# Strassen's scheme for the first FFN product beside attention, with weight sums streamed from DRAM

## The chip, the cores and the metric

One core of a Trainium2 chip. The metric is the device time of one execution, in microseconds (us), of that core. I write PE for TensorE, ACT for ScalarE, DVE for VectorE, POOL for GpSimd and SP for SyncE, as the profile does.

## The reference

Attention with a threshold over 8 sequences of 8 heads (576 x 64), then a feed-forward network (FFN) with ELU on the 4608 tokens, all in fp32:

```python
scores = scale * np.matmul(q, k.transpose(0, 1, 3, 2))
thresh = np.max(scores, axis=-1, keepdims=True) - tau
scores = np.where(scores >= thresh, scores, -1000000000.0)
attn = np.exp(scores - np.max(scores, axis=-1, keepdims=True))
attn = attn / (np.sum(attn, axis=-1, keepdims=True) + 1e-09)
attn_out = np.matmul(attn, v)
# ... (heads are put side by side: x is 4608 x 512)
h = x @ w_in                                        # 512 -> 2048
g = np.where(h > 0.0, h, np.exp(np.minimum(h, 0.0)) - 1.0)
return g @ w_out                                    # 2048 -> 512
```

## The kernel before

Heads are worked in pairs, 32 of them (four per sequence). The FFN of a group of 512 finished tokens fills PE while the attention of later pairs waits for softmax. A pair has five steps. In each, PE makes scores; DVE takes the maximum, ACT the exponential, DVE masks and sums, POOL normalizes; DVE turns 32 x 32 squares of the weights into a tile `x`, and SP writes it to DRAM and reads it back as the transposed weights for the product with v.

```python
    def turn_squares(pr, i):
        w = open_steps.pop((pr, i))["w"]
        x = late["x"].tile([P, NT, NCH, T], FP32, name="x", bufs=2)
        # ... (DVE: nc.vector.transpose, 3 to 4 times)
        there = turns[pr, i] = dram.tile([NT, T, NT, NCH * T], FP32, name="there")
        for p in range(NT):
            nc.sync.dma_start(there[:, :, p]..., x[p * T : (p + 1) * T]...)
```

Beside attention the first FFN product is plain: 4 matmuls into a bank, and only then exponential, minus one, ELU.

```python
        def part(k):
            ft = fts[k]
            if k == 0:
                loc["ph"] = psum["f"].tile([P, 2, CT], FP32, name="ph", tag="f")
            for j in range(KJ):
                nc.tensor.matmul(loc["ph"][:, k], w_in_sb[:, j, ft * P : (ft + 1) * P],
                                 xts[g][:, j, hf * CT : (hf + 1) * CT], start=(j == 0), stop=(j == KJ - 1))
```

The second product uses Strassen's scheme (7 products of half-blocks in place of 8, for some additions) already. In the final stage, after attention, both products do.

## Time and profile before

| | before |
|---|---|
| time, median of 3 (range) | 1424.34 us (1419.48 to 1424.73) |
| span of the profiled execution | 1418.1 us |
| PE busy / idle | 1373.6 / 44.5 us |
| a pair of heads beside attention, pairs 11 to 30, alternately | 37.7 and 38.6 us |
| moved by DMA | 204 MB, 144 GB/s |

The idle time is the span less PE's busy time. A pair is measured from the start of its first scores to that of the next pair's; the "pairs" below alternate between those in which the changed kernel does a first product ("first pairs") and a second product ("second pairs"). One more line of the page matters, the chain that ended last, followed back from the end:

```profile
PE 84%; DVE 8%; ACT 3%; POOL 2%; issue 2%; SPq 0%; DMA 0%; DVEq 0%; POOLq 0%
```

A chain that is 84% PE says that nearly everything else lay beside PE's work.

### The profile page before, as it was taken

Reading aid. Unit: us, or ns where it says so; the run is one execution under the profiler, and the core shown is the slowest. Engines: PE = TensorE matmul, PEld = TensorE weight load, DVE = VectorE, ACT = ScalarE, POOL = GpSimd, SP = SyncE. Lnnn points to the kernel's source line nnn. Section 1 sums busy time; section 2 is a strip of 40 time slices with the busy share of each in tenths; the row PEclk is TensorE's granted clock in tenths of the full one; section 3 lists DMA queues with packets and bytes.
Section 4 is the critical chain, followed back from the end, with each engine's and each line's share of the span. In section 5 each row is a group of like instructions: output and inputs, shape, how many; then the busy total and the mean of one; then the engine's idle time right before and its main releaser. Section 6 shows DMA issues by size and latency. Waiting matters only on the chain.

```text
span 1418.1 us, 20448 instructions
## 1 busy us (share of the span) xinstructions
PE 1373.6 (97%) x6758; PEld 1024.1 (72%) x6758; DVE 950.5 (67%) x2070; ACT 449.2 (32%) x812; POOL 669.4 (47%) x1170
## 2 busy tenths in 40 slices
PE   6897989999999999999999999999999999999998
PEld 4455645657777777777777777777777777788887
DVE  6878884667676767676776767676767767563542
ACT  5676654223232322232232323232323222120220
POOL 5566774646363544545353626354544445241330
PEclk9999999999999999999999999999999999999999
DMA  5254451567666767767676767667776765100001
GB/s 112 56 98 138 127 145 41 142 166 189 188 188 181 192 183 192 193 184 184 180 190 180 193 183 192 183 183 189 192 193 170 201 174 170 59 0 15 15 1 30
DMA packets 298905, 205.45 MB, mean 145 GB/s; under 512 B 206384, under 2 KB 270384, under 8 KB 298800
## 3 DMA queue, kind: packets, MB, share of 16 engines
q1 hardware_dynamic: 298800, 204.15, 53.9%
q8 instruction: 54, 0.88, 0.3%
q14 instruction: 51, 0.42, 0.1%
HBM read 119.87 MB, written 84.21 MB: 144 GB/s over the span
## 4 chain that ended last, share of the span: by engine, by line
PE 84%; DVE 8%; ACT 3%; POOL 2%; issue 2%; SPq 0%; DMA 0%; DVEq 0%; POOLq 0%
PE ph L434 26%; PE po L539 24%; PE sc L236 12%; PE pv L386 9%; PE po L868 7%; DVE w L263 3%; ACT e L251 3%; PE po L503 2%; PE pv L382 2%; DVE mx L246 2%; PE rt L275 1%; POOL wtop L142 1%; DVE wtop L136 1%; POOL nb L247 1%; DVE wtop L135 1%
## 5 line engine op out<-in xcount | busy, mean ns | idle before, releaser
L434 PE MATMUL ph<-xt,w_in_sb 128*128 128x256 f32 x1792 | 406.7, 382 | 0.0
L434 PEld LDWEIGHTS ph<-xt,w_in_sb 128*128 128x128 f32 x1792 | 335.2, 190 | 64.0 <-issue 20.5
L251 ACT ACTIVATE e<-sc,nb,keep 128x576 f32<-128x576 f32 x288 | 227.4, 829 | 473.6 <-POOL nb L247 472.6
L246 DVE TENSOR_REDUCE mx<-sc 128x2 f32<-128x1152 f32 (+1 forms) x176 | 199.7, 1136 | 234.6 <-PE sc L236 234.6
L272 POOL TENSOR_SCALAR w<-w,rs 128x576 f32<-128x576 f32 x288 | 224.3, 789 | 224.7 <-DVE rs L266 216.8
L263 DVE SCALAR_TENSOR_TENSOR w<-sc,th,e 128x576 f32<-128x576 f32 x288 | 226.2, 815 | 78.5 <-ACT e L251 54.9
L236 PE MATMUL sc<-kT,qT 64*128 64x288 f32 x1024 | 181.1, 439 | 22.4 <-DVE w L263 12.0
L346 DVE STREAM_TRANSPOSE x<-w 128x512 f32<-128x512 f32 (+1 forms) x350 | 181.1, 566 | 0.9 <-POOL w L272 0.9
L247 POOL TENSOR_SCALAR nb<-mx,nkeep 128x2 f32<-128x2 f32 (+1 forms) x176 | 51.2, 291 | 261.7 <-DVE mx L246 253.8
L236 PEld LDWEIGHTS sc<-kT,qT 64*128 64x128 f32 x1024 | 99.9, 190 | 87.3 <-issue 52.4
L539 PE MATMUL po<-t,s 128*128 128x256 f32 x512 | 122.8, 386 | 4.5 <-DVE u L559 4.5
L539 PE MATMUL po<-w_out_sb,s 128*128 128x256 f32 x512 | 120.1, 384 | 0.0
L539 PEld LDWEIGHTS po<-t,s 128*128 128x128 f32 x512 | 94.6, 190 | 28.9 <-DVE u L559 8.9
L539 PEld LDWEIGHTS po<-w_out_sb,s 128*128 128x128 f32 x512 | 95.4, 190 | 19.7 <-issue 4.7
L442 ACT ACTIVATE g<-ph 128x512 f32<-128x512 f32 x112 | 66.9, 597 | 126.0 <-PE ph L434 126.0
L539 PE MATMUL po<-w_out_sb,g 128*128 128x256 f32 x448 | 103.2, 379 | 0.0
L445 POOL TENSOR_SCALAR g<-g 128x512 f32<-128x512 f32 x112 | 70.0, 625 | 66.8 <-ACT g L442 65.8
L539 PEld LDWEIGHTS po<-w_out_sb,g 128*128 128x128 f32 x448 | 85.1, 190 | 12.2
L449 DVE SCALAR_TENSOR_TENSOR g<-g,ph 128x512 f32<-128x512 f32 x112 | 74.8, 669 | 18.2 <-POOL g L445 18.1
L471 POOL TENSOR_TENSOR s<-g 128x256 f32<-128x256 f32 x112 | 82.7, 739 | 3.9 <-DVE g L912 3.9
L386 PE MATMUL pv<-wTb,vm 128*64 128x320 f32 x512 | 78.1, 448 | 0.0
L393 ACT COPY xt<-pv 128x256 f32<-128x256 f32 x64 | 23.8, 371 | 155.5 <-PE pv L386 155.5
(161 smaller groups left out, 1512.7 us busy)
## 6 DMA issues: line engine op xcount, KB each, us to landing
there<-x SPq DMA_DIRECT2D x500, 144.0 KB, 3.4
wTb<-there SPq DMA_DIRECT2D x75, 576.0 KB, 4.5
wTa<-there SPq DMA_DIRECT2D x50, 576.0 KB, 3.7
qm<-in_q_dram SPq DMA_DIRECT2D x128, 72.0 KB, 2.7
km<-in_k_dram SPq DMA_DIRECT2D x128, 72.0 KB, 3.7
vm<-in_v_dram SPq DMA_DIRECT2D x64, 128.0 KB, 2.5
wst<-in_moe_w_in_dram SPq DMA_DIRECT2D x16, 512.0 KB, 4.6
wst<-in_moe_w_out_dram SPq DMA_DIRECT2D x16, 512.0 KB, 4.2
```

Source lines behind the costliest of these rows:

```text
L236: nc.tensor.matmul(scs[h][:, a, :HALF], qs[r], kT[r, k0 : k0 + HALF], start=True, stop=True)
L246: nc.vector.tensor_reduce(st["mx"][:, cs], src[:, :, :, :HALF], axis=AX.XY, op=ALU.max)
L251: nc.scalar.activation(e, st[h][:, :, :HALF], AF.Exp, bias=st["nb"][:, h : h + 1], scale=keep)
L263: nc.vector.scalar_tensor_tensor(wv, sc[:, :, :HALF], st["th"][:, h : h + 1], e, ALU.is_ge, ALU.mult, accum_out=sm[:, h : h + 1])
L272: nc.gpsimd.tensor_scalar(wv, wv, st["rs"][:, h : h + 1], 1.0, ALU.mult, ALU.mult)
L346: nc.vector.transpose(x[:, :, c0 : c0 + nc_], src.rearrange("p (c g n) -> p g c n", c=nc_, n=T))
L386: nc.tensor.matmul(pv[h * D : (h + 1) * D, g0 * T : g1 * T], vm[:, h, c], wT[:, g0:g1, h * (NC + 1) + c], start=False, stop=(c == NC - 1), ...
L434: nc.tensor.matmul(loc["ph"][:, k], w_in_sb[:, j, ft * P : (ft + 1) * P], xts[g][:, j, hf * CT : (hf + 1) * CT], start=(j == 0), stop=(j = ...
L449: nc.vector.scalar_tensor_tensor(loc["g"], loc["g"], 0.0, loc["ph"], ALU.min, ALU.max)
L471: engines[k].tensor_tensor(out, x, y, op)
L539: nc.tensor.matmul(cur[c, place], lhs, rhs, start=(begins and u == 0), stop=(u == NU - 1), skip_group_check=True)
L868: nc.tensor.matmul(place, left[:, k], right[:, k], start=(begins and k == 0), stop=(k == 1), skip_group_check=True)
```

## The change

The intent: 7 products instead of 8 in the first product beside attention as well. Sums of weight blocks are made once, written to DRAM and loaded again per unit, since there is no room for them. To save room the hidden features are done in two rounds of half of them. ACT copies three products out of PSUM in each unit, POOL and DVE add them, and an agenda sorted by planned time replaces the fixed order. Maxima, biases and exponentials go by head instead of by pair, with the bias of the exponential on ACT. The diff, cut:

```diff
     def turn_squares(pr, i):
         w = open_steps.pop((pr, i))["w"]
-        x = late["x"].tile([P, NT, NCH, T], FP32, name="x", bufs=2)
+        x = late["x"].tile([P, NT, NCH, T], FP32, name="x", bufs=1)
...
+            def product(k):
+                # ... (three banks; s: the sums loaded from DRAM)
+                left, right, place, begins = ((s[:, 0], x1, 0, True), (s[:, 1], b22, 1, True), (s[:, 2], b11, 2, True),
+                                              (a11, b12, 1, False), (a22, b21, 2, False), (a21, x6, 1, False),
+                                              (a12, x7, 0, False))[k]
+                for j in range(2):
+                    nc.tensor.matmul(loc["banks"][place], left[:, j], right[:, j], start=(begins and j == 0), stop=(j == 1),
+                                     skip_group_check=True)
...
+            after_ = (
+                [(0.1, lambda: copy("s1", 0))],
+                [(0.1, lambda: copy("w1", 1))],
+                [(0.1, lambda: copy("u2", 2)), ... (POOL sums) ...],
+                [(0.1, lambda: nc.scalar.copy(h(0, 1), place(1)))],
+                [(0.1, lambda: nc.scalar.copy(h(1, 0), place(2))), ...],
+                [(0.1, lambda: add(h(1, 1), 1, "s1")), *tail(1)],
+                [(0.1, lambda: add(h(0, 0), 0, "t5")), *tail(0)],
+            )            # tail(c): exp at +0.7 (ACT), minus one at +1.45 (POOL), ELU at +2.2 (DVE)
...
+        def softmax(pr, i):
+            t = clock[0]
+            on_pe(1.25, lambda: scores(pr, i, hs))
+            for h in hs:
+                at(t + 1.2 + 0.01 * h, lambda h=h: max_of(pr, i, h))
+                at(t + 2.0 + 0.75 * h, lambda h=h: bound_of(pr, i, h))
+                at(t + 2.1 + 0.8 * h, lambda h=h: exp_of(pr, i, h))
+                at(t + 3.1 + 0.85 * h, lambda h=h: mask_of(pr, i, h))
+            # ... (reciprocal, normalize)
+            at(t + 6.2, lambda: turn_squares(pr, i))
...
```

## The prediction

> **What bounds the kernel now.** I read the page first, its shares and its costliest groups:
>
> ```profile
> PE 1373.6 (97%) x6758; PEld 1024.1 (72%) x6758; DVE 950.5 (67%) x2070; ACT 449.2 (32%) x812; POOL 669.4 (47%) x1170
> ...
> L434 PE MATMUL ph<-xt,w_in_sb 128*128 128x256 f32 x1792 | 406.7, 382 | 0.0
> ...
> L251 ACT ACTIVATE e<-sc,nb,keep 128x576 f32<-128x576 f32 x288 | 227.4, 829 | 473.6 <-POOL nb L247 472.6
> ...
> L471 POOL TENSOR_TENSOR s<-g 128x256 f32<-128x256 f32 x112 | 82.7, 739 | 3.9 <-DVE g L912 3.9
> ```
>
> PE is busy 97% of the span. The costliest group is the plain first product, and no idle time stands before it. Then I read the busy times by stretch, over ten whole pairs of heads (from one transpose of kT to the tenth after it, so one pair takes 38.14 us):
>
> ```profile
> 312.50:693.90 381.40, 379.18 (x1921) 286.97 (x1922) 266.43 (x580) 108.12 (x180) 183.99 (x344) 1.00 0.69 187
> ```
>
> The columns are length, busy time of PE, weight loads, DVE, ACT and POOL, the granted clock, the DMA share and GB/s. PE idles 2.2 us in 381, so beside attention the time is PE's. DVE works 26.6 us per pair, ACT 10.8, POOL 18.4. Third, the timeline of one attention step, because the change puts work on ACT and DVE that PE waits for:
>
> ```profile
> 603.14 1.24 PE L236 MATMUL sc<-kT,qT 64*128 64x288 f32 x8
> ...
> 604.31 1.99 PE L539 MATMUL po<-t,s 128*128 128x256 f32 x8
> 604.42 1.36 DVE L246 TENSOR_REDUCE mx<-sc 128x2 f32<-128x1152 f32 x1 [3.27 <-PE sc L236]
> ...
> 605.88 0.27 POOL L247 TENSOR_SCALAR nb<-mx,nkeep 128x2 f32<-128x2 f32 x1 [3.40 <-DVE mx L246]
> ...
> 606.18 1.55 ACT L251 ACTIVATE e<-sc,nb,keep 128x576 f32<-128x576 f32 x2 [7.40 <-POOL nb L247]
> ```
>
> PE has left the scores 1.17 us after it began them, the maximum starts 1.28 us after, one engine follows another in about 0.1 us, and ACT then does two exponentials in 1.55 us without a gap. Today nothing on PE needs ACT in that time. Fourth, the final stage, which already runs Strassen's first product, with ACT free:
>
> ```profile
> 1226.14 1.03 PE L868 MATMUL po<-xt,w_in_sb 128*128 128x256 f32 x4
> ...
> 1227.01 1.03 PE L868 MATMUL po<-wTa,w_in_sb 128*128 128x256 f32 x4
> 1227.21 0.37 ACT L874 COPY s<-po 128x256 f32<-128x256 f32 x1 [0.56 <-PE po L868]
> ...
> 1227.87 1.03 PE L868 MATMUL po<-xt,w_in_sb 128*128 128x256 f32 x4
> ```
>
> The three PE rows are one product each (two matmuls, four records). They start 0.865 us apart, so a matmul of 256 columns costs 0.432 us. A bank can be read 1.07 us after its product began, a copy takes 0.37, and PE's next product in that bank, two products on, began 0.29 us after the copy ended. That is the whole slack of such a bank, and it needs an idle ACT.
>
> [...] I therefore count matmuls by their spacing (0.432 us). The trace agrees that busy time is not work: it gives 1792 records 382 ns each, which start about 216 ns apart. [...] The trace of before agrees: three banks hold three independent units and L434 idles 0.0. The change lets the seven products of one unit return to the same three banks. [...] here it is 0.73 us in the steady stretch against 0.42 on DVE for 256 columns.
>
> **The change, part by part.**
>
> PE, removed. A group of 512 tokens needs 128 matmuls in the first product, and by Strassen 8 units x 7 products x 2 = 112. Six groups lie beside attention (groups 7 and 8 used the scheme already): 6 x 16 x 0.432 = 41.5 us, or 1.7 us per pair, 3.4 us per two pairs. The count of the second product stays (two rounds of half its depth). If PE stayed the bound, the time were 1383.
>
> Engines, added per pair (a quarter of a group). DVE: 30 more additions of 256 columns per group (16 in the first product, 14 from the second in two rounds), 7.5 x 0.42 = 3.1; input sums 1.25 x 0.69 = 0.9; maxima by head 9 x 0.75 against 4 x 1.36 + 0.75, 0.6; ELU from SBUF, 0.4. Sum 5, so 31.5 us of 36.4: 86%. ACT: 10 copies x 0.37 = 3.7, nine small bias products x 0.2 = 1.8; 16.5 us. POOL: 7.5 x 0.73 = 5.5; 24 us. No engine passes PE on the average.
>
> Waits, added: this decides. Each unit writes banks 0, 1, 2, 1, 2, 1, 0. Before products 3, 4 and 5 ACT must have copied products 1, 2 and 3 out, each with the 0.29 us of slack above. Engines take instructions in program order, and the agenda sorts ACT's by planned time. A pair of heads is planned with 8, 6, 4, 6, 4 quarters (one product each) in its five steps, 28, exactly four units. So the phase is the same in each first-product pair, and I can write it out. With 0 at the scores' start: maximum of head 0 at 1.29 to 2.04, bias on ACT 2.14 to 2.34, exponential of head 0 to 3.19, then copy s1 to 3.5, bias and exponential of head 1 to 4.5, then copy w1 to 4.9. PE starts product k at 1.17 + 0.86 k.
> - Steps 0 and 2 (products 0 to 3 follow the scores): product 3 would start at 3.75, and must wait for w1 till about 5.0: 1.25 us each.
> - Step 1 (products 1, 2, 3, 4 first): product 3 waits for a copy behind the exponential of head 0, 3.6 against 2.9; product 4 for one behind that of head 1, 5.0 against 4.5: 1.25 together.
> - Step 3 begins with product 4, whose copies have time: 0. Step 4 begins with product 3, and product 5 waits for a copy behind its only exponential: 0.75.
> Sum 4.5 us per first-product pair, with a DVE that is never late. Half of the 24 pairs are such: 12 x 4.5 = 54 us, more than the 41.5 saved.
>
> On top, chosen rather than read off: an ELU that stands in DVE's order before the next maximum waits for POOL, which normalizes (2 x 0.75) before it serves the unit's sums. Written out for step 1 the maximum comes about 1.1 us late, and each such delay reaches PE through the exponentials. I take 1.5 us per first-product pair, 18 us. In second-product pairs, sums of the last unit queue on POOL behind the normalization: 0.5 us, 6 us. Two pairs between the stages in which PE has only the plain chunk while POOL and DVE make weight sums: 4 us. The final stage has as many matmuls as before and idled little (PE 48.5 of 50 us where it begins), so 0.
>
> Sum: 1424 - 41.5 + 54 + 18 + 6 + 4 = 1464.5, I say 1465.
>
> DMA: the sums of w_in are 128 x 768 x 4 bytes = 0.39 MB a unit, those of w_out 128 x 1024 x 4 bytes x 6 = 3.1 MB a group: 6.3 MB per group, 41 GB/s over 152 us on 187. Each is asked for several products ahead, in rows of 3 to 4 KB. I expect no PE wait on them.
>
> **Rivals.**
> 1. PE stays the bound and most of the 41.5 us arrives: 1385 to 1396. For it: the averages (DVE 86%, ACT 46%), scores in two banks by head, which ends the wait for the mask, and an order planned by time. Against it: the written-out steps, which use only durations of this trace and the program's order.
> 2. Only the floor of waits happens, DVE and POOL never add to it: 1424 - 41.5 + 54 = 1437, within 2%. For it: PE's stalls give the other engines time to catch up, so lateness cannot pile up.
> 3. DVE becomes the bound in first-product pairs: there it has 8 additions and 8 ELUs per pair rather than the mean, so about 33 us of work, and waits for POOL and ACT in its order. Then each step grows by about 2 us, and the time passes 1500. For it: I carried one whole first-product pair on paper this way and lost nearly 9 us. Against it: lateness of 1 us often falls where PE has slack.
> 4. DMA becomes late (its share goes from 0.69 to about 0.8, mostly packets below 512 B). A wait for the turned weights would stand before pv; 10 us more. I give it little.
>
> **Range and chances.** The floor is the firmest part, and it is just above the time before. So faster than 1396 needs the copies to escape the exponentials: 0.12. Up to 1453 needs the floor with little on top: 0.30. Above it: 0.58. The range, 1405 to 1515, reaches from half the floor to rival 3.
>
> **What would show it.** Right: PE's busy share beside attention falls to about 90%; idle stands before first-product matmuls, ended by ACT copies (s1, w1, u2 or the copies into g), twice as much in every other pair; ACT's copies wait behind exponentials; first-product pairs take 40 us or more and second-product pairs about 37. The first product's records fall by 6 x 32 = 192. Wrong: PE at 98% with pairs of 36.5 us (rival 1); PE idle ended by DVE additions, not ACT copies (rival 3); idle before pv ended by DMA (rival 4).

The 0.73 and 0.42 us are one addition of 256 columns on POOL and on DVE: over 312.5 to 693.9 us of the trace of before, the sums of L471 took 731 ns each on POOL; those of L876, in the final stage, 422 to 425 ns on DVE.

## The result and the profile after

| | before | after |
|---|---|---|
| median of 4 runs (range) | 1421.92 us (1419.48 to 1424.73) | 1617.37 us (1613.14 to 1622.12) |
| profiled execution: span | 1418.1 | 1620.3 |
| PE busy / idle | 1373.6 / 44.5 | 1412.3 / 208.0 |
| until pair 9 / pairs 9 to 30 / from pair 31 on | 319.3 / 839.0 / 259.8 | 328.1 / 1012.9 / 279.3 |
| first pairs / second pairs (mean of 10) | 37.7 / 38.6 | 52.8 / 38.6 |
| half-rate records of PE's clock, sum | 18.1 us | 169.8 us |

The ratio of the fast runs is 1.1375 (95% interval 1.1332 to 1.1417). The last row adds up the stretches that the trace records with PE's clock at 0.5; each lasts 3.41 us or a multiple of it, but for the last one, which every trace here has at its end and which runs past the span by 2.0 us.

The page of the changed kernel, its busy times, the chain that ended last, and the groups where PE and DVE stand:

```profile
PE 1412.3 (87%) x6566; PEld 1022.5 (63%) x6566; DVE 1080.5 (67%) x2362; ACT 603.9 (37%) x1323; POOL 872.0 (54%) x1395
...
PE 50%; DVE 14%; ACT 9%; POOL 8%; SPq 7%; issue 7%; DMA 5%; DVEq 0%; POOLq 0%; ACTq 0%
...
L348 DVE STREAM_TRANSPOSE x<-w 128x512 f32<-128x512 f32 (+1 forms) x350 | 188.3, 575 | 95.2 <-DMA there<-x 71.9
...
L839 PE MATMUL f<-xt,w_in_sb 128*128 128x256 f32 x512 | 148.7, 431 | 69.5 <-ACT w L853 67.2
...
L839 PE MATMUL f<-x,w_in_sb 128*128 128x256 f32 x448 | 132.0, 447 | 53.8 <-ACT g L888 53.8
```

Three things are to be seen. First, 192 records are gone and yet PE is busy for longer. Second, PE's idle time stands before first-product matmuls that wait for ACT copies (121.0 us in the two groups), as predicted; but the chain that ended last is now half other engines, with 12% in SP's queue and DMA. Third, the transposes into `x` wait 71.9 us for the write `there<-x`. The same group of before:

```profile
L346 DVE STREAM_TRANSPOSE x<-w 128x512 f32<-128x512 f32 (+1 forms) x350 | 181.1, 566 | 0.9 <-POOL w L272 0.9
```

That wait comes from the first hunk of the diff, which my prediction passed over. How it reaches PE is seen in one step, from the changed kernel's timeline of a first pair, step 0 (start, length, what, and in brackets how long its engine had stood idle and what ended that):

```profile
606.50 1.97 SPq L361 DMA_DIRECT2D there<-x  x4
...
607.77 1.24 PE L238 MATMUL sc<-kT,qT 64*128 64x288 f32 x8
...
609.91 1.89 PE L839 MATMUL f<-xt,sw 128*128 128x256 f32 x8
612.30 1.30 DVE L348 STREAM_TRANSPOSE x<-w 128x512 f32<-128x512 f32 x2 [5.68 <-DMA there<-x]
...
613.78 1.38 DVE L1026 TENSOR_REDUCE mx<-sc 128x1 f32<-128x576 f32 x2
...
614.86 0.83 ACT L1036 ACTIVATE e<-sc,nb,keep 128x576 f32<-128x576 f32 x1
...
616.91 0.36 ACT L853 COPY w<-f 128x256 f32<-128x256 f32 x1
...
617.33 3.78 PE L839 MATMUL f<-xt,w_in_sb 128*128 128x256 f32 x8 [5.53 <-ACT w L853]
```

The scores were there at 609.0. In DVE's order the transposes of the step before stood ahead of the maximum, and they had no buffer until the write before them had landed. SP had begun to issue that write at 606.50, though its transposes had ended at 602.6; loads of q and v (599.78 to 606.39) stood before it in SP's order. That is only a part of the wait: over the 23 waits for the write in this trace, it began 2.7 us after the transposes on the average, its four issues took 2.5 us, and the last landed 2.7 us later. So the maximum came at 613.78, then the exponentials, and behind them in ACT's order the copy of a product that had been ready since about 611. PE waited 5.53 us. And its next four matmuls (eight records) took 3.78 us instead of 1.89: the trace records the clock at 0.5 from 616.27 on.

Step 4 of the same pair loses as much without any write:

```profile
647.81 1.91 POOL L274 TENSOR_SCALAR w<-w,rs 128x576 f32<-128x576 f32 x2
...
650.11 0.62 POOL L869 TENSOR_SCALAR ge<-ge 128x512 f32<-128x512 f32 x1
...
650.76 1.20 DVE L873 SCALAR_TENSOR_TENSOR g<-ge,g 128x512 f32<-128x512 f32 x1 [1.66 <-POOL ge L869]
...
651.88 1.48 DVE L348 STREAM_TRANSPOSE x<-w 128x512 f32<-128x512 f32 x3
653.30 0.71 DVE L1026 TENSOR_REDUCE mx<-sc 128x1 f32<-128x576 f32 x1
...
654.37 0.83 ACT L1036 ACTIVATE e<-sc,nb,keep 128x576 f32<-128x576 f32 x1
655.10 0.36 ACT L888 COPY g<-f 128x256 f32<-128x256 f32 x1
...
655.52 3.78 PE L839 MATMUL f<-x,w_in_sb 128*128 128x256 f32 x8 [4.52 <-ACT g L888]
```

It is one thread through four engines: POOL normalizes before it takes the ELU's minus one, DVE's ELU waits for that, the transposes and the maximum stand behind the ELU, and the copy PE waits for stands behind the exponential. The scores had been ready at 649.3.

**Where the 202.2 us between the two profiled spans came from.** The matmuls removed are worth -41.5 (the prediction's count). PE's idle time rose by 163.5, of which the two copy groups are 121.0, the waits of the second product for POOL's sums 17.8, and one wait of 11.4 at the start of the stage. Busy time rose by 38.7 in spite of the removal, so by 80.2. In half-rate stretches PE was busy 142.5 us after and 13.3 before; if half of that is what the halving cost, it is 71 against 7, an estimate of 64 of the 80.

### The profile page after: what moved, and what is told of

It is laid out like the page before. It is cut to its first block, busy times and chain, and to the rows that moved or that the text cites. A ratio compares the mean times of both kernels' runs of the same rounds, so it can differ in the third digit from the quotient of the medians.

```text
span 1620.3 us, 21836 instructions
## 1 busy us (share of the span) xinstructions
PE 1412.3 (87%) x6566; PEld 1022.5 (63%) x6566; DVE 1080.5 (67%) x2362; ACT 603.9 (37%) x1323; POOL 872.0 (54%) x1395
## 3 DMA queue, kind: packets, MB, share of 16 engines
q1 hardware_dynamic: 316512, 259.21, 61.3%
## 4 chain that ended last, share of the span: by engine, by line
PE 50%; DVE 14%; ACT 9%; POOL 8%; SPq 7%; issue 7%; DMA 5%; DVEq 0%; POOLq 0%; ACTq 0%
PE f L954 16%; PE f L839 13%; PE sc L238 7%; PE pv L388 6%; DMA there<-x 4%; DVE x L348 3%; ACT e L1036 3%; DVE mx L1026 3%; SPq L179 2%; POOL w L274 2%; PE pv L384 2%; POOL s L914 2%; SPq L361 2%; ACT nb L1034 2%; PE f L475 2%
## 5 line engine op out<-in xcount | busy, mean ns | idle before, releaser
L348 DVE STREAM_TRANSPOSE x<-w 128x512 f32<-128x512 f32 (+1 forms) x350 | 188.3, 575 | 95.2 <-DMA there<-x 71.9
L238 PE MATMUL sc<-kT,qT 64*128 64x288 f32 x1024 | 185.8, 442 | 27.5 <-DVE w L265 17.8
L839 PE MATMUL f<-xt,w_in_sb 128*128 128x256 f32 x512 | 148.7, 431 | 69.5 <-ACT w L853 67.2
L1034 ACT ACTIVATE nb<-mx,nkeep 128x1 f32<-128x1 f32 x207 | 60.9, 294 | 371.3 <-DVE mx L1026 371.3
L839 PE MATMUL f<-x,w_in_sb 128*128 128x256 f32 x448 | 132.0, 447 | 53.8 <-ACT g L888 53.8
L839 PEld LDWEIGHTS f<-xt,w_in_sb 128*128 128x128 f32 x512 | 103.6, 212 | 108.4 <-ACT w L853 81.7
L1026 DVE TENSOR_REDUCE mx<-sc 128x1 f32<-128x576 f32 x207 | 146.6, 744 | 37.9 <-PE sc L238 37.7
L839 PEld LDWEIGHTS f<-x,w_in_sb 128*128 128x128 f32 x448 | 101.3, 229 | 76.4 <-ACT g L888 58.6
L839 PE MATMUL f<-xt,sw 128*128 128x256 f32 x512 | 127.1, 388 | 1.6 <-DVE g L861 0.2
L954 PE MATMUL f<-t,s 128*128 128x256 f32 x448 | 109.7, 383 | 17.8 <-POOL s L914 17.8
L954 PE MATMUL f<-w_out_sb,s 128*128 128x256 f32 x448 | 107.5, 383 | 7.2 <-DVE t L963 7.1
L839 PEld LDWEIGHTS f<-xt,sw 128*128 128x128 f32 x512 | 96.5, 192 | 23.7 <-DVE g L861 7.3
L954 PE MATMUL f<-w_out_sb,g 128*128 128x256 f32 x448 | 109.5, 387 | 0.0
```

Source lines behind the costliest of these rows:

```text
L238: nc.tensor.matmul(scs[h][:, a, :HALF], qs[r], kT[r, k0 : k0 + HALF], start=True, stop=True)
L348: nc.vector.transpose(x[:, :, c0 : c0 + nc_], src.rearrange("p (c g n) -> p g c n", c=nc_, n=T))
L839: nc.tensor.matmul(loc["banks"][place], left[:, j], right[:, j], start=(begins and j == 0), stop=(j == 1), skip_group_check=True)
L954: nc.tensor.matmul(loc["banks"][place], lhs, rhs, start=(begins and v == 0), stop=(v == RU - 1), skip_group_check=True)
L1026: nc.vector.tensor_reduce(st["mx"][:, h : h + 1], st[h][:, :, :HALF], axis=AX.XY, op=ALU.max)
L1034: nc.scalar.mul(st["nb"][:, h : h + 1], st["mx"][:, h : h + 1], nkeep)
```

## The experiments

My theory after the result: (A) the single buffer makes DVE late in step 0; (B) the order of DVE (ELU, then transposes, then the maximum) makes it late in step 4; (C) copies that stand behind exponentials on ACT pass this lateness on to PE; (D) long pauses of PE halve its clock on top: from 612.86 to 616.27 us, inside the 5.53 us above, PE was busy 0.00 us at a clock of 1.00, and the next 6.82 us are at 0.5. The rivals: that it is only the floor of copies behind exponentials, as predicted; that POOL or DVE simply have too much work; and that the clock is a consequence of something other than the pauses.

All kernels gave correct results. Each was run once, beside one run of the kernel before on the same chip, so differences of a few us say nothing: the kernel before's own runs differ by 5 us, those of the changed kernel by 9. The kernel before took 1420.45, 1420.13, 1423.31 and 1424.11 us in the four batches. Step means are over pairs 11 to 30.

| run | us | against before, same batch | PE busy | PE idle | half-rate, us | first / second pair |
|---|---|---|---|---|---|---|
| after | 1617.37 | +195.5 | 1412.3 | 208.0 | 169.8 | 52.8 / 38.6 |
| x2 | 1548.17 | +127.7 | 1379.3 | 167.1 | 95.5 | 47.4 / 37.9 |
| dve | 1619.25 | +198.8 | 1413.1 | 204.4 | 161.1 | 50.3 / 41.6 |
| act | 1600.87 | +180.4 | 1408.4 | 190.7 | 133.2 | 46.3 / 43.0 |
| x2_act | 1530.93 | +110.8 | 1384.9 | 144.3 | 92.1 | 40.6 / 42.7 |
| x2_dve | 1506.16 | +86.0 | 1371.7 | 132.7 | 58.2 | 43.3 / 38.4 |
| x2_dve_act | 1484.98 | +64.9 | 1375.2 | 108.0 | 64.9 | 38.5 / 41.3 |
| all4 | 1469.34 | +49.2 | 1367.1 | 100.5 | 54.2 | 38.4 / 40.5 |
| all5 | 1458.92 | +35.6 | 1363.0 | 94.1 | 26.6 | 38.5 / 39.8 |
| order_only | 1586.81 | +162.7 | 1396.6 | 188.4 | 121.7 | 46.6 / 42.8 |
| before_x1 | 1444.14 | +20.8 | 1381.0 | 61.3 | 36.4 | 39.6 / 38.8 |
| gap4 | 1443.39 | +20.1 | 1378.8 | 62.8 | 18.8 | as before |
| gap9 | 1504.38 | +83.9 | 1407.1 | 95.2 | 85.6 | as before |

### x2: the second buffer put back

The room came from one buffer of hidden sums, so what x2 gains is net of what that costs.

```diff
-        x = late["x"].tile([P, NT, NCH, T], FP32, name="x", bufs=1)
+        x = late["x"].tile([P, NT, NCH, T], FP32, name="x", bufs=2)
-                    cur[g, r, c, k] = late["x"].tile([P, RU, P], FP32, name=f"s{k}", bufs=2 if k < 2 else 1)
+                    cur[g, r, c, k] = late["x"].tile([P, RU, P], FP32, name=f"s{k}", bufs=2 if k < 1 else 1)
... (the sums that then wait for this buffer are let go after product m == 3)
```

> The changed kernel with the buffer of the turned weights (x) doubled again, as the kernel before has it; the space comes from one buffer of the sums s2. Theory A (the single x makes DVE wait for the write of the step before, and everything behind it in DVE's order is late): the waits of DVE's transposes for that write, 72 us in the changed kernel, fall below 10 us, step 0 of the first-product pairs falls from about 14 us to about 10, and the time to about 1510 us. Rival B (the order on ACT and DVE is what costs, the buffer only adds a little): the wait moves to another place and the time stays above 1590 us.

Some 68 us less, where about 107 were expected. Step 0 of the first pairs fell from 14.4 to 9.8 us, the wait for the write from 71.9 to 1.2. Step 4 stayed (13.7 to 13.3). From the waits of x2 (engine, line, what it waited for: total us, times, longest):

```profile
PE f L839 <- ACT g L888: 49.7, 12, 4.2
PE f L839 <- ACT w L853: 39.7, 35, 1.7
...
DVE x L348 <- DMA there<-x: 1.2, 1, 1.2
```

Here the floor of the prediction stands alone: in the second row, 35 waits for the copy w1, three per first pair, 1.13 us each, where it said 1.25 in steps 0, 1 and 2. The first row is step 4: 4.1 us each, where it said 0.75 and 1.5 for lateness.

### dve: the maxima ahead of the transposes and the ELU

```diff
-                at(t + 1.2 + 0.01 * h, lambda h=h: max_of(pr, i, h))
+                at(t + 0.05 + 0.01 * h, lambda h=h: max_of(pr, i, h))
-                return [(0.7, lambda: exp(c)), (1.45, lambda: minus(c)), (2.2, lambda: elu(c))]
+                return [(0.7, lambda: exp(c)), (1.45, lambda: minus(c)), (3.6, lambda: elu(c))]
-            at(t + 6.2, lambda: turn_squares(pr, i))
+            at(t + 6.6, lambda: turn_squares(pr, i))
```

> Only DVE's order: maxima planned at the start of the scores, ELU 1.4 us later and the turned weights 0.4 us later than before, so that in the short steps the maxima stand ahead of both. Theory B (order on DVE): step 4 of the first-product pairs, 13 us in the changed kernel, falls to about 8, step 0 stays at 13 to 15, the time is about 1555 us. Theory A: DVE's maxima are late because of the buffer, and this moves the time by less than 20 us.

Missed: no gain at all. Step 4 fell from 13.7 to 7.7, so (B) is right there. But step 0 grew by 1.6, step 2 by 3.1 and the second pairs by 2.9 us; DVE's wait for the write grew from 71.9 to 98.5. With one buffer, the better order in one step is paid for in the others.

### act: the exponentials 1.75 us apart, with copies between them

```diff
-                at(t + 2.1 + 0.8 * h, lambda h=h: exp_of(pr, i, h))
-                at(t + 3.1 + 0.85 * h, lambda h=h: mask_of(pr, i, h))
+                at(t + 2.25 + 1.75 * h, lambda h=h: exp_of(pr, i, h))
+                at(t + 3.25 + 1.75 * h, lambda h=h: mask_of(pr, i, h))
```

> Only ACT's order: the exponentials are planned 0.15 us (first head) and 1.1 us (second head) later, masks and normalization with them, so that the copies that PE waits for stand ahead of the second exponential, and in steps 1 and 4 ahead of both. Theory C (PE waits because copies stand behind exponentials in ACT's order, whatever makes those late): PE's idle time ended by ACT's copies, 121 us in the changed kernel, is halved, step 4 of the first-product pairs goes from 13 to about 7 us, step 1 from 7.6 to 6.8, the time to about 1500 us. Rival: the copies only change places with the exponentials, masks come later, and PE waits for the masks instead: within 20 us of 1617.

Missed by 100 us, and inside the 20 us that the rival allowed. Step 4 did fall to 6.8 and step 0 to 8.7, but step 1 rose from 8.9 to 13.7 and the second pairs from 38.6 to 43.0. PE's wait for the copy w1 fell from 67.2 to 15.4, and that for the copy into g vanished from the largest waits. In their place PE now waited 55.7 us for DVE's additions and 30.3 for its ELUs, while DVE waited 99.9 us for the write, more than the 71.9 of the changed kernel. So ACT's order was where the lateness of DVE reached PE, and not its source.

### gap9: pauses put into the kernel before

Nine more copies of the first sum in each unit of the final stage, where nothing else is short. Its matmuls are the same.

```diff
             product(a11, b11, X, True)
+            for _ in range(9):
+                kept("s1", X)
             p1 = kept("s1", X)
```

> The kernel before, in whose final stage (16 units of Strassen's first product, nothing else on ACT) nine more copies of the first product hold its bank, so PE pauses once a unit. Theory D (a pause of PE itself costs, and then the granted clock is halved for some microseconds): pauses of about 2.9 us each, 46 us in all, granted clock in that stage well below 1.00, and the time grows by 60 to 80 us. Rival: the granted clock stays at 1.00 there and the time grows by the pauses alone, 40 to 50 us.

It took 83.9 us more: PE idle rose by 50.7, in 16 waits of up to 3.3 us for the copies, and PE busy by 33.5, for the same matmuls.

```profile
PE po L868 <- ACT s L874: 50.8, 16, 3.3
```

The windows of one such pause, cut at the edges of the half-rate record (columns: length, busy PE, weight loads, DVE, ACT, POOL, granted clock, DMA share, GB/s):

```profile
1231.29:1234.70 3.41, 1.01 (x5) 0.56 (x3) 0.00 (x0) 2.98 (x8) 0.34 (x1) 1.00 0.00 0
1234.70:1238.11 3.41, 2.57 (x6) 2.12 (x7) 1.02 (x2) 1.65 (x4) 0.92 (x1) 0.50 0.00 0
1238.11:1241.53 3.42, 3.42 (x9) 2.70 (x9) 0.89 (x3) 0.00 (x0) 0.00 (x0) 0.50 0.00 0
1241.53:1244.94 3.41, 3.26 (x15) 2.52 (x14) 3.12 (x8) 1.54 (x4) 0.87 (x1) 1.00 0.00 0
```

In the first window PE was busy 30% of the time, and the next one is at half rate. In that one it was busy 75%, and the rate stays. After a full window the rate is back. So (D) is shown, in the final stage, without any of the change's other parts. The estimate used above (half of PE's busy time in half-rate stretches, 36.6 us here less 6.7 before) gives 29.9 for the 33.5 measured.

### x2_act, x2_dve, x2_dve_act and all4: the mends together

The edits are those above, together. The last also issues the first loads and the first input sums before the stage begins:

```diff
+            if n in (MIDDLE - 2, MIDDLE - 1):
+                load_in(n - MIDDLE + 2)
+            if n == MIDDLE - 1:
+                # ... (the input sums of group 1, from the stage's first step)
```

> The two x buffers of run x2, and ACT's order of run act on top. Theory C: with DVE no longer waiting for the write, the copies ahead of the exponentials take most of what is left: PE's idle time ended by ACT's copies (89 us in x2) falls below 35, step 4 of the first-product pairs from 13 to about 7 us, the pair from 47.4 to about 40, the time to about 1460. Rival E (the lateness only moves to DVE's additions, which stand behind the same transposes and maxima, as in run act where PE waited 56 us for them): above 1510.

> The two x buffers and DVE's order of run dve on top. Theory B: step 4 falls from 13 to about 8 us, the pair to about 42.5, the time to about 1490. Rival: alone, this order gave nothing (1619 against 1617), and what it takes from step 4 it gives to step 0 and to the second product, which waits for the later ELU: within 20 us of 1548.

> All three. If the two orders are independent causes: about 1445. If both only take the same lateness from different ends: no better than the better one of the two by more than 15 us. Half-rate time of the clock, 96 us in x2, falls below 50 us[...].

> All three, and the start of the stage prepared earlier: the first two weight sums and the first input sums are fetched and made before the last step of the stage before. The start of the stage costs about 20 us in one step of pair 9 (21.6 us in x2, where 8 would do): 10 to 14 us less than x2_dve_act.

The first three were slower than expected, by 71, 16 and 40 us. In x2_act the first pairs fell to 40.6 as expected and PE's waits for ACT's copies to 35.6, but the time was that of rival E (above 1510). In x2_dve_act the two orders were neither independent (1445) nor the same thing (within 15 us of x2_dve): it gained 21, and its half-rate time was 64.9 us, not below 50. all4 gained 15.6 on the three mends, where 10 to 14 were expected. With two buffers the order on DVE, worth nothing alone, is worth 42 (127.7 to 86.0). The order on ACT is worth 17 or 21 and moves time from the first pairs (43.3 to 38.5) into the second (38.4 to 41.3): exponentials planned later make masks and ELUs later, and the second product waits for g. That is what PE waits for longest in x2_act, and in x2_dve_act it is still 25.2 us:

```profile
PE f L954 <- DVE g L873: 30.2, 12, 3.8
```

### before_x1: the single buffer alone, in the kernel before

```diff
-        x = late["x"].tile([P, NT, NCH, T], FP32, name="x", bufs=2)
+        x = late["x"].tile([P, NT, NCH, T], FP32, name="x", bufs=1)
   (and two plain tiles in the final stage for the second buffer that it borrowed there)
```

> The kernel before with the one line of the change that the prediction passed over: one buffer instead of two for the weights that are turned, written to DRAM and loaded again (and two plain buffers in the final stage in place of the second one there). If a single buffer costs what it cost beside the change (about 70 us with the kernel after), because it makes VectorE late by itself, 1470 to 1495 us. If it costs only where TensorE's next product waits for something that VectorE or ScalarE releases soon after, as in the changed kernel's steps 0, then here, where the FFN product of these steps was enough steps ahead, less: 1425 to 1450 us, with VectorE waiting for the write there<-x just as long as in the changed kernel.

The second: 20.8 us, with the same wait on DVE as in the changed kernel.

```profile
L346 DVE STREAM_TRANSPOSE x<-w 128x512 f32<-128x512 f32 (+1 forms) x350 | 181.5, 568 | 69.6 <-DMA there<-x 69.1
```

69.1 us of waiting here and 71.9 in the changed kernel; 21 us of time here, 68 there. Only the second has copies on ACT that PE needs within a microsecond.

### gap4: shorter pauses

As gap9, with four copies.

> The kernel before with 4 more copies of the first sum in each of the 16 final units (9 in gap9, whose pauses of some 3 us halved the granted clock). Pauses of 1.1 to 1.5 us in the same place. [...] the time rises by the pauses alone: 18 to 26 us, busy time of TensorE unchanged within 3 us, granted clock 1.00 in the final stage. If any pause costs clock in proportion (gap9: 33 us of clock to 51 us of pauses), another 12 to 16 us of busy time, 1452 to 1462 us.

The first: 20.1 us, the pauses.

```profile
PE po L868 <- ACT s L874: 18.2, 15, 1.3
```

PE's busy time rose by 5.2, more than the 3 allowed, but the half-rate stretches sum to 18.8 us against 18.1, and from 300 us on there is none but that at the very end. So these pauses, of 1.3 us at most, cost no clock here. They do cost a little more than themselves: from pair 31 on, PE was busy 258.2 us against 253.9 for the same matmuls at full clock, 4.3 us in 16 pauses or 0.27 each.

### all5: all mends, and another order in the second pairs

```diff
-                ... (3.6, lambda: elu(c))]
+                ... (3.6 if v < RU - 1 else 2.2, lambda: elu(c))]
-            ... for m in range(7) for k in range(2)]
+            turns_ = [(0, 0), (1, 0), (0, 1), (1, 1)] + [(m, k) for m in range(2, 7) for k in range(2)]
+            ... for m, k in turns_]
-                at(t + 2.25 + 1.75 * h, lambda h=h: exp_of(pr, i, h))
+            e0, e1 = (4.0, 4.9) if i == 2 else (2.25, 4.0)
+                at(t + (e1 if h else e0), lambda h=h: exp_of(pr, i, h))
-            at(t + 6.6, lambda: turn_squares(pr, i))
+            at(max(t + 6.6, m + 0.35), lambda: turn_squares(pr, i))
```

> The version with all four mends (1469 us), its second products and exponentials set in another order: the last unit's ELU 1.4 us earlier, the second product's first two quarters each followed by the other feature half's work, both exponentials of step 2 later, the turned weights behind the reciprocal. If what is left beside attention is lateness that order can remove (a pair with the second product 40.5 us, step 0 of it 11.3 against about 8.1 of matmuls), 15 to 30 us less than all4: 1440 to 1455 us. If it is the room of VectorE and ScalarE itself, no gain: 1462 to 1478 us. In no case under the kernel before's 1420.

Between the two: 1458.92 us, 10 to 14 less than all4. The half-rate time of the stage is nearly gone (26.6 us, 18.1 of it in the kernel before as well). PE is still idle 94.1 us against 44.5. The largest of its waits in the stage are now small ones of every kind:

```profile
PE f L960 <- DVE g L879: 12.3, 12, 1.9
PE f L845 <- DMA sw<-win_sums: 8.4, 7, 3.0
...
PE f L960 <- DVE t L969: 7.6, 5, 1.8
PE f L845 <- DVE g L867: 7.4, 21, 0.4
PE f L960 <- ACT s L965: 6.1, 11, 0.6
```

No version beat the kernel before.

### order_only: all5 with the single buffer again

```diff
-        x = late["x"].tile([P, NT, NCH, T], FP32, name="x", bufs=2)
+        x = late["x"].tile([P, NT, NCH, T], FP32, name="x", bufs=1)
   (and the hidden sums' buffers as the change had them)
```

> The version of 1459 us (all5) with the change's single buffer for the turned weights put back (and the first-sum buffers as the change had them): every mend but the buffer. In the kernel before, the single buffer made VectorE wait 69 us and the time rise by 21; in the changed kernel, where copies for TensorE queue behind what VectorE releases, it was worth 69 to 72. If the better order of ScalarE and VectorE frees TensorE from that coupling, as before: 1475 to 1490 us. If the coupling stays, since the maximum of step 0 still stands behind the late turned weights: 1515 to 1545 us, most of it in step 0 of the pairs and in copies for the first product, with pauses that halve the clock.

The coupling stays, and more strongly than expected: 1586.81 us. From its timeline, step 0 of a first pair, whose scores PE began at 592.66:

```profile
600.43 1.31 DVE L348 STREAM_TRANSPOSE x<-w 128x512 f32<-128x512 f32 x2 [8.65 <-DMA there<-x]
...
603.73 0.36 ACT L859 COPY w<-f 128x256 f32<-128x256 f32 x1
...
604.14 3.78 PE L845 MATMUL f<-xt,w_in_sb 128*128 128x256 f32 x8 [7.45 <-ACT w L859]
```

So the buffer is worth 68 us in the change's own order (+195.5 to +127.7) and 127 in the mended order (+162.7 to +35.6); the other mends are worth 33 with one buffer and 92 with two. The mended order plans the transposes later, which suits two buffers; with one, DVE waits 105.6 us for the write (71.9 in the change's order). The two causes are not a sum: whichever is left makes DVE late, and lateness on DVE is what PE pays for.

## Why the prediction was wrong

The direction was right and the size far off: 1465 against 1617, outside the range of 1405 to 1515. By its own steps:

- **PE, removed.** 192 records left, as counted. The worth of 41.5 can't be read back from PE's busy time, which rose.
- **The floor in steps 0 to 2.** Right in mechanism and nearly in size: 1.13 us per wait in x2. It was no floor of the hardware, though: with the exponentials apart, PE's waits for the copy w1 fell from 43.9 us in x2_dve to 11.7 in x2_dve_act. One of its terms, 0.2 us for the bias on ACT, was my guess, from no trace; it took 0.29 (L1034 of the changed kernel, 294 ns).
- **Step 4 and the lateness.** This mechanism, an ELU ahead of the maximum in DVE's order that waits for POOL's normalization, was in the prediction; the sizes were wrong. The terms 0.75 and 1.5 measured 4.5 (53.8 us in 12 waits), and lateness hit step 4, not step 1, for which I had written it out. I had counted the ELU's wait but not the transposes that stand between it and the maximum, 1.48 us, nor that the ELU itself took 1.20. I also had a better number and did not use it: rival 3 says that one whole first pair, carried through on paper, lost nearly 9 us, and the sum took 4.5 + 1.5. In x2, with the buffer back, the first pairs took 47.4 us, 11 above the 36.4 of a pair without waits.
- **What the sum left out: the buffer.** The step that failed is "Waits, added". It lists waits for banks and for late work, and none for the tile `x`, although the diff takes one of its two buffers away. It is worth 68 us alone and 127 behind the other mends. The premise "with a DVE that is never late" fell with it.
- **What the sum left out: the clock.** Every pause was counted once, at its length. In the changed kernel long ones were followed by half-rate matmuls as well (after that of 5.53 us, four matmuls took 3.78 us instead of 1.89): some 64 us in all, an estimate. I had counted none of that, since the clock before stood at 1.00 beside attention (312.50 to 693.90 us).
- **Program order.** "Engines take instructions in program order" is the core of it, and the timeline shows it for DVE and ACT: the maximum of 613.78 had its scores at 609.0 and stood behind the transposes of 612.30, which had lacked a buffer for 5.68 us; the copy of 616.91 had its product since about 611 and stood behind the exponentials of 614.86 and 616.18.
- **Second pairs.** 38.6 us on the average, where about 37 was predicted; the waits for POOL's sums were 17.8, not 6. Right in kind.
- **Between and after.** The start of the stage cost 11.4 us in one wait (4 predicted), and the end from pair 31 on 19.5 us, about half of it idle PE and half busy time, where I said 0; the final products themselves did not stall. I did not follow up that end: in all5 it is still 11.
- **The rivals.** Rivals 1 and 2 lay far below the measured time. Rival 3 put DVE as the bound: its time passes 1500, but DVE is busy 67% of the span and 65% of the first pairs; it is late, not full. That POOL or DVE have too much work can't be the cause of most of the loss: in all5 the same work on the same engines takes 158 us less. Rival 4 was right in that the turned weights' transfers matter, and wrong in the place: not the read before the product with v, but the write that frees the buffer. PE waited for loads of `sw` for 8.4 us in all in all5; where the start had not been prepared, the first wait alone took 10.9 to 12.1.

What stays open. Fully mended as far as I got, the change still loses 36 us. PE's idle is 50 above the kernel before's. Its busy time is 31 above what the removed matmuls should leave (1373.6 - 41.5 = 1332.1 against 1363.0), of which the clock explains about 4 (half of 26.6 less 18.1, by the same estimate). For the other 27, gap4 gives an estimate: each wait cost 0.27 us of busy time there, and after the start of pair 9 PE waits 71 times in all5 for more than 0.15 us and 103 times for more than 0.05, against 15 before, which makes 15 to 24. The same count for the changed kernel (82 waits) gives 18, where the clock left 16 of the 80 unexplained. No run shows it in this stage. What sets the rate is not shown either: after 1231.29 us in gap9 it fell when PE had been busy 1.01 of 3.41 us, but from 15.52 to 29.17 us of the changed kernel it stood at 0.5 with PE busy for all 13.65 us. The idle time sits mostly in the second pairs: in all5 PE is idle 1.2 us of a first pair's 38.5 and 2.6 us of a second pair's 39.8. That the plan of the additions can't be fitted in is not shown either; only that these orders don't do it.

## What to carry to other kernels

When PE depends on other engines within a microsecond, follow each queue back in program order: here what a wait cost was set by the work that stood behind it in the queue, and not by the instruction that waited (5.68 us on DVE in step 0 became 5.53 on PE, by way of ACT). A buffer that is taken away for room must be costed as a wait, with the queue that issues its release: this one made DVE wait 69.1 us in before_x1 and 71.9 in the changed kernel, where SP began the write 2.7 us after its data were ready, and it was worth 21 and 68 us of time. And look at the clock after PE's pauses: those of gap9, 3.3 us at the longest, came with 33.5 us more of busy time on 50.7 of pause; those of gap4, 1.3 us at the longest, with no more half-rate time than before (18.8 us against 18.1).
